# An attention and gated-convolution kernel: one convolution moved to other banks, one pair of loads moved forward, three output stores held back

## The chip, the cores and the metric

The kernel runs on one core of one Trainium2 chip. The metric is the device time of one execution in microseconds (us); the median of several executions is quoted, and a profile of one execution stands beside it. An execution counts as slow when it is over 1.5% above the fastest of the same kernel. Of all executions below only two of the kernel before, in the third call of the experiments (226.51 and 227.51 us), were slow; the ratios leave them out.

## The reference

Causal attention over 8 batches, 12 heads, 448 positions and 64 features per head, followed by a gated unit: a causal convolution of width 5 over each of the 768 features gives a gate, a dense product gives a value, and their product goes through an output projection.

```python
scores = scale * q @ k.T ; masked above the diagonal ; attn = softmax(scores)
x = (attn @ v) as [8, 448, 768]
gate = sigmoid(sum(conv_w[k] * x shifted by 4 - k for k in range(5)))
out  = (gate * (x @ w_val)) @ w_out        # float32 [8, 448, 768]
```

## The kernel before

The 96 heads are worked through as 24 groups of four (three groups to a batch). Everything is unrolled, and each engine is given its instructions in the order in which the program issues them. PSUM is the memory into which the matmuls write; the copy of a finished bank from there into an output tile, done by ACT, is called an eviction below. It is split by hand: two double banks for scores (`sc_ps`), two for attention values (`av_ps`), one for denominators (`den_ps`) and one more (`z_ps`); projections and value products borrow the last two.

```python
qk_pool = ctx.enter_context(tc.tile_pool(name="qk", bufs=QK_BUFS))     # 5
ob_pool = ctx.enter_context(tc.tile_pool(name="ob", bufs=4))           # output tiles
...
def load_v(n):            # on SP; buffer n % 3, so it waits for the cast of group n - 3
...
def conv(units, banks):   # 40 matmuls per group, then a tanh on ACT out of the banks
...
def project(p, m, half, o, tiles):
    if half == 0:
        obs[p, m] = ob_pool.tile([128, DM], FP32, name="ob")
    ob = obs[p, m]
    ...                                             # 6 or 24 matmuls into bank o
        nc.scalar.activation(out=ob[:, f], in_=o[:, 0:384], func=AF.Copy, scale=0.5)
    ...
    elif half == 1:
        nc.sync.dma_start(out=rows, in_=ob)         # 384 KB, on SP
...
def first_half(n):
    exps(n, 0)              # scores (PE), exponentials (ACT), masks (POOL)
    transposes(n + 1)       # q and k of the next group (DVE)
    cast_v(n)               # POOL
    load_v(n + 3)           # SP
    for m in {4: (6, 7), 5: (8,), 6: (9,), 7: (10, 11)}.get(n, (n + 4,)):
        load_qk(m)          # POOL's queue
...
for p in range(2, N // 2 + 1):        # two groups a turn; fill[] says how many
    n = 2 * p                         # half output tiles go into each gap
    first_half(n)
    gap(0, (den_ps, z_ps))
    second_half(n)                    # exps(n, 1)
    values(n - 1)                     # attention values (PE), normalisation (DVE)
    gap(1, (z_ps,), 4)
    ...
    first_half(n + 1)
    gap(2, (den_ps, z_ps))
    second_half(n + 1)
    if n < N:
        values(n)
    gap(3, (z_ps,), 4)
    conv((n - 2, n - 1) if p > 2 else (n - 1,), sc_banks)
    gap(4, (den_ps, z_ps, av_ps[0]))
```

In the turn p = 2 the gaps hold output tiles 0 and 1, in p = 3 tile 2, and in p = 4 tile 3's first half (gap 1), then tile 3's second half and tile 4's first half (both in gap 2), then tile 4's second half (gap 3).

The softmax here doesn't subtract the row's maximum and nothing guards it: scores larger than these inputs give would overflow.

## Time and profile before

| what | value |
|---|---|
| time, median of 3 runs (range) | 224.27 us (223.78 to 224.67) |
| span of the profiled execution | 222.6 us |
| TensorE busy | 208.4 us, 94% |
| idle of TensorE from 38.5 to 66.9 us | 2.9 us |
| idle of TensorE from 98 to 194 us | 0.1 us |
| ACT, DVE, POOL busy | 63%, 63%, 50% |

A busy share is an average over the whole span. What a change is worth is read from the stage that it touches: there TensorE either waits, and can gain, or it does not. The lines for this are in the prediction. In such lines PE is TensorE, ACT ScalarE, DVE VectorE, POOL GpSimd, and SPq the queue of SyncE, which issues the loads of v and all stores. The two leading numbers are the start and the duration in us, and a bracket gives an idle time of the engine and what ended it.

### The profile page before, as it was taken

How to read it: one execution, taken by the hardware profiler on the slowest of the kernel's cores; microseconds unless marked ns; L12 is line 12 of the kernel's file. 1: busy time of each engine (PE TensorE's matmuls, PEld its weight loads, DVE VectorE, ACT ScalarE, POOL GpSimd, SP SyncE). 2: the span in 40 equal slices, each digit the busy share in tenths (PEclk: the TensorE clock that was granted, in tenths of full speed). 3: DMA queues.
4: the chain of work that ended last, by engine and by line, in shares of the span. 5: the costliest groups of instructions: out<-in, count | busy, mean ns of one | idle time of the engine just before them, and what ended most of it. 6: DMA issues, size and time to landing. Idle time of an engine off the chain costs nothing.

```text
span 222.6 us, 8748 instructions
## 1 busy us (share of the span) xinstructions
PE 208.4 (94%) x3821; PEld 114.1 (51%) x3822; DVE 139.4 (63%) x251; ACT 139.7 (63%) x178; POOL 111.4 (50%) x192
## 2 busy tenths in 40 slices
PE   7997889987999999999999999999999999989992
PEld 3344434544455545545655655555555556546551
DVE  6747686558878754978828828749568476260400
ACT  2496316877666868667677777777677776406041
POOL 7299953893884736817717636557255155000000
PEclk9999699999999999999999999999999999999999
DMA  5999999899999885984885977758934210302333
GB/s 92 176 196 223 220 215 203 169 171 268 223 271 203 172 180 209 239 157 90 161 235 109 229 212 134 154 192 165 193 141 135 88 59 3 144 0 89 128 137 149
DMA packets 57696, 36.37 MB, mean 163 GB/s; under 512 B 46133, under 2 KB 54069, under 8 KB 57658
## 3 DMA queue, kind: packets, MB, share of 16 engines
q1 hardware_dynamic: 48922, 22.44, 37.6%
q0 software_dynamic: 8736, 13.37, 34.6%
q8 instruction: 30, 0.49, 0.9%
q14 instruction: 8, 0.07, 0.1%
HBM read 37.76 MB, written 11.01 MB: 219 GB/s over the span
## 4 chain that ended last, share of the span: by engine, by line
PE 77%; ACT 8%; DVE 7%; DMA 3%; issue 2%; POOL 1%; DVEq 0%; ACTq 0%; POOLq 0%
PE den_ps L263 12%; PE z_ps L263 11%; PE sc_ps L181 11%; PE z_ps L285 11%; ACT pt L190 7%; PE sc_ps L241 7%; PE den_ps L285 6%; PE av_ps L215 5%; PE den_ps L215 4%; PE av_ps L285 3%; PE z_ps L134 3%; DMA kb<-in_k_dram 3%; PE sc_ps L285 2%; DVE x L228 2%; DVE dt L222 1%
## 5 line engine op out<-in xcount | busy, mean ns | idle before, releaser
L190 ACT ACTIVATE pt<-sc_ps 128x1024 bf16<-128x1024 f32 x96 | 92.9, 1022 | 34.1 <-PE sc_ps L181 32.6
L194 POOL TENSOR_SCALAR_AFFINE_SELECT pt<-pt 128x512 bf16<-128x512 bf16 x24 | 16.0, 668 | 66.5 <-ACT pt L190 66.5
L285 PEld LDWEIGHTS <-gv 128*32 128x32 bf16 (+1 forms) x624 | 31.6, 97 | 22.3 <-issue 4.6
L263 PEld LDWEIGHTS <-wv 128*128 128x128 bf16 x288 | 26.4, 98 | 26.0 <-issue 3.2
L181 PE MATMUL sc_ps<-qt,kt 32*128 32x64 bf16 (+3 forms) x768 | 35.0, 277 | 2.1 <-ACT pt L190 1.6
L285 PE MATMUL z_ps<-wo,gv 128*32 128x384 bf16 (+1 forms) x462 | 33.2, 326 | 0.8 <-DVE gv L266 0.8
L200 POOL TENSOR_SCALAR_AFFINE_SELECT pt<-pt 128x512 bf16<-128x512 bf16 x48 | 30.2, 660 | 7.0 <-ACT pt L190 7.0
L181 PEld LDWEIGHTS <-kt 32*128 32x128 bf16 x768 | 18.4, 93 | 27.4 <-issue 17.2
L263 PE MATMUL z_ps<-x,wv 128*128 128x448 bf16 x138 | 30.2, 353 | 0.7 <-DVE x L228 0.7
L263 PE MATMUL den_ps<-x,wv 128*128 128x448 bf16 x138 | 30.3, 354 | 0.2
L266 DVE SCALAR_TENSOR_TENSOR gv<-gate,den_ps 128x448 bf16<-128x448 f32 x23 | 14.1, 612 | 24.6 <-PE den_ps L263 24.6
L228 DVE TENSOR_TENSOR x<-av_ps,rb 128x448 bf16<-128x448 f32 x48 | 27.7, 619 | 2.6
L248 ACT ACTIVATE gate<-sc_ps 128x896 f32<-128x896 f32 x23 | 19.9, 915 | 14.9 <-PE sc_ps L241 14.9
L222 DVE STREAM_TRANSPOSE dt<-den_ps 128x448 f32<-128x448 f32 x24 | 15.5, 644 | 18.4 <-PE den_ps L215 18.4
L215 PE MATMUL av_ps<-pt,vb 128*32 128x448 bf16 (+3 forms) x768 | 25.3, 274 | 0.7 <-DVE vb L86 0.7
L165 DVE STREAM_TRANSPOSE qt<-qb 128x448 uint32<-128x448 uint32 x24 | 22.8, 950 | 4.7 <-DMA qb<-in_q_dram 4.5
L290 ACT ACTIVATE ob<-z_ps 128x384 f32<-128x384 f32 x29 | 14.3, 493 | 15.8 <-PE z_ps L285 15.8
L165 DVE STREAM_TRANSPOSE kt<-kb 128x448 uint32<-128x448 uint32 x24 | 22.3, 930 | 1.8 <-DMA kb<-in_k_dram 1.8
L86 POOL CAST vb<-vf 128x1024 bf16<-128x1024 f32 x21 | 21.8, 1036 | 0.0
L215 PEld LDWEIGHTS <-vb 128*32 128x32 bf16 x768 | 16.3, 98 | 6.4 <-DVE vb L86 0.9
L241 PE MATMUL sc_ps<-x,cwd 32*32 32x448 bf16 x920 | 17.7, 369 | 1.8 <-DVE x L228 0.9
L266 DVE SCALAR_TENSOR_TENSOR gv<-gate,z_ps 128x448 bf16<-128x448 f32 x23 | 14.1, 614 | 7.9 <-PE z_ps L263 7.9
(46 smaller groups left out, 174.9 us busy)
## 6 DMA issues: line engine op xcount, KB each, us to landing
out_dram<-ob SPq DMA_DIRECT2D x27, 384.0 KB, 4.1
vf<-in_v_dram SPq DMA_DIRECT2D x72, 128.0 KB, 5.6
qb<-in_q_dram POOLq DMA_DIRECT2D x24, 224.0 KB, 4.8
kb<-in_k_dram POOLq DMA_DIRECT2D x24, 224.0 KB, 6.0
vf<-in_v_dram SPq DMA_DIRECT2D x24, 64.0 KB, 5.3
wv<-in_moe_w_val_dram POOLq DMA_DIRECT2D x12, 96.0 KB, 6.0
wo<-in_moe_w_out_dram POOLq DMA_DIRECT2D x6, 192.0 KB, 8.8
wv<-wv SPq DMA_DIRECT2D x4, 96.0 KB, 7.6
```

The source lines that it names most:

```text
L86: engine.tensor_copy(out=t, in_=vfs.pop(n))
L165: nc.vector.transpose(out=t.bitcast(U32).rearrange("p (b s) -> p s b", s=T), in_=qks.pop((name, n)).rearrange("p s d -> p (s d)").bitcast( ...
L181: nc.tensor.matmul(out=sc_ps[h // 2][:, h % 2, c0:c0 + nq], lhsT=kt[r, e, k0:k0 + 128], rhs=qt[r, e, q0:S], start=e == 0, stop=e == 1, ski ...
L190: nc.scalar.activation(out=pt[:, 2 * hp:2 * hp + 2, 512 * stage:512 * (stage + 1)], in_=sc_ps[hp], func=AF.Exp, scale=D ** -0.5)
L200: nc.gpsimd.affine_select(out=pt[:, :, c:c + 128], in_=pt[:, :, c:c + 128], compare_op=ALU.is_ge, fill=0.0, base=0, pattern=[[0, G], [1, 1 ...
L215: nc.tensor.matmul(out=o, lhsT=w, rhs=pt[:, h, col:col + nq], start=i == 0, stop=i == 3, skip_group_check=True, tile_position=(0, 32 * i_out))
L228: nc.vector.tensor_tensor(out=x[:, dh, 4:S + 4], in0=av_ps[dh][:, 0:S], in1=r, op=ALU.mult)
L241: nc.tensor.matmul(out=banks[u][i // 2][32 * j:32 * (j + 1), 0:S], lhsT=cwd[r, 2 * version(n) + dh, t], rhs=xs[n % 8][r, dh, t:t + S], sta ...
L248: nc.scalar.activation(out=gates[n], in_=sc_ps[u][:, :, 0:S], func=AF.Tanh, scale=0.5)
L263: nc.tensor.matmul(out=o[e][:, 0:S], lhsT=wv_sb[version(NG * b + cg)][:, ce, f:f + 128], rhs=xs[(NG * b + cg) % 8][:, ce, 4:S + 4], start= ...
L266: nc.vector.scalar_tensor_tensor(out=gv[g][:, e, S * (b % 2):S * (b % 2 + 1)], in0=gates[NG * b + g][:, e], scalar=1.0, in1=o[e][:, 0:S], ...
L285: nc.tensor.matmul(out=o[w * j:w * (j + 1), 0:384], lhsT=gvs[p][g][:, dh, 128 * m + w * j:128 * m + w * (j + 1)], rhs=wo_sb[c][:, f], star ...
```

## The change

Three things at once, all aimed at the early stage where TensorE still waits: the convolution of group 3 runs in the two value banks, ahead of group 4's values, so that the projection after it no longer needs `den_ps`; q and k of group 6 are asked for before a cast on POOL; and the stores of output tiles 0, 1 and 2 are held until tile 3 is complete, to leave the DMA queues to the loads.

```diff
@@ -271,6 +271,13 @@
     obs = {}
+    stores = []
+
+    def store():
+        while stores:
+            rows, ob = stores.pop(0)
+            nc.sync.dma_start(out=rows, in_=ob)
+
@@ -294,7 +301,9 @@
         elif half == 1:
-            nc.sync.dma_start(out=rows, in_=ob)
+            stores.append((rows, ob))
+            if p > 0 or m > 2:
+                store()
@@ -324,7 +333,7 @@
-            for m in {4: (6, 7), 5: (8,), 6: (9,), 7: (10, 11)}.get(n, (n + 4,)):
+            for m in {4: (7,), 5: (8,), 6: (9,), 7: (10, 11)}.get(n, (n + 4,)):
@@ -384,6 +393,7 @@
     conv((2,), [av_ps])
     exps(3, 1)
+    load_qk(6)
     cast_v(3)
@@ -412,11 +422,14 @@
         second_half(n + 1)
+        if p == 2:
+            conv((n - 1,), [av_ps])
         if n < N:
             values(n)
         gap(3, (z_ps,), 4)
-        conv((n - 2, n - 1) if p > 2 else (n - 1,), sc_banks)
-        gap(4, (den_ps, z_ps, av_ps[0]))
+        if p > 2:
+            conv((n - 2, n - 1), sc_banks)
+        gap(4, (den_ps, z_ps, av_ps[0]) if p > 2 else (z_ps,))
```

(Some unchanged lines around the edits are cut.)

## The prediction

> **What bounds the kernel now.** I read the page first: part 1 and the PE row of part 2.
>
> ```profile
> PE 208.4 (94%) x3821; PEld 114.1 (51%) x3822; DVE 139.4 (63%) x251; ACT 139.7 (63%) x178; POOL 111.4 (50%) x192
> ...
> PE   7997889987999999999999999999999999989992
> ```
>
> TensorE is busy for 208.4 of 222.6 us. The row shows that what it loses, it loses early (the first ten slices of 5.6 us) and in the tail. So a part of the change can gain only where TensorE waits early, and anything that stops TensorE in the dense middle is added in full.
>
> Second, the timeline of PE from 44 to 53 us, where groups 4 and 5 run and the convolution of group 3 stands:
>
> ```profile
> 46.88 0.63 PE L181 MATMUL sc_ps<-qt,kt 32*128 32x320 bf16 x14 [0.60 <-ACT pt L190]
> 47.44 0.62 PE L215 MATMUL den_ps<-pt,ones 128*32 128x448 bf16 x16
> 47.89 1.05 PE L215 MATMUL av_ps<-pt,vb 128*32 128x448 bf16 x32
> 48.87 1.14 PE L241 MATMUL sc_ps<-x,cwd 32*32 32x448 bf16 x40
> 51.21 1.14 PE L285 MATMUL den_ps<-wo,gv 128*128 128x384 bf16 x6 [1.20 <-DVE dt L222]
> 52.28 0.64 PE L181 MATMUL sc_ps<-qt,kt 32*128 32x448 bf16 x16
> ```
>
> One projection waits 1.20 us for the bank den_ps, because DVE had not yet read group 4's denominators. The timeline of DVE gives the reason:
>
> ```profile
> 48.37 0.98 DVE L165 STREAM_TRANSPOSE qt<-qb 128x448 uint32<-128x448 uint32 x1 [1.90 <-DMA qb<-in_q_dram]
> 49.75 0.95 DVE L165 STREAM_TRANSPOSE kt<-kb 128x448 uint32<-128x448 uint32 x1 [0.41 <-DMA kb<-in_k_dram]
> 50.56 0.60 DVE L222 STREAM_TRANSPOSE dt<-den_ps 128x448 f32<-128x448 f32 x1
> ```
>
> The transposes of group 6's q and k stand ahead of that read in DVE's order. They waited for loads that POOL issued only at 43.35 and 43.89, behind two casts. This is the wait the change aims at.
>
> Third, since held stores keep buffers, the timelines of ACT and then of SP at the place where the stores will now be issued:
>
> ```profile
> 75.36 0.50 ACT L290 ACTIVATE ob<-den_ps 128x384 f32<-128x384 f32 x1
> 75.73 0.51 ACT L290 ACTIVATE ob<-z_ps 128x384 f32<-128x384 f32 x1
> 76.12 1.95 ACT L190 ACTIVATE pt<-sc_ps 128x1024 bf16<-128x1024 f32 x2
> ```
>
> ```profile
> 77.61 2.00 SPq L78 DMA_DIRECT2D vf<-in_v_dram  x3
> 79.66 0.61 SPq L79 DMA_DIRECT2D vf<-in_v_dram  x1
> 80.80 2.69 SPq L297 DMA_DIRECT2D out_dram<-ob  x3
> ```
>
> By the plan of the loop, the evictions at 75.36 and 75.73 are the second half of output tile 3 and the first half of tile 4. The store of tile 3 was ready at 75.86, yet SP issued it at 80.80: it stood behind the loads of v for group 12, which wait for POOL's cast of group 9 (76.55 to 77.59 in the timeline of POOL).
>
> [...] a ready store stood 4.9 us behind a waiting load. [...] Here the store of 80.80 took 5.6 us to land, against a median of 4.1 for the 27 stores. [...] one ACT eviction that waits holds the exponentials behind it. No wait in this trace tests that on ACT; DVE shows the same (above). [...] The table by stage agrees: after TensorE had been only 0.29, 0.79, 0.56 and 0.40 busy in the four microseconds from 20 on, it shows
>
> ```profile
> 24.00:25.00 1.00, 1.00 (x48) 0.70 (x57) 1.00 (x1) 0.00 (x0) 1.00 (x3) 0.50 1.17 216
> 25.00:26.00 1.00, 1.00 (x43) 0.39 (x30) 0.00 (x0) 0.00 (x0) 1.00 (x2) 0.50 1.20 198
> 26.00:27.00 1.00, 1.00 (x27) 0.63 (x24) 0.00 (x0) 0.90 (x2) 1.00 (x3) 0.50 1.14 207
> ```
>
> The value 0.50 is the granted clock. Dense work resumed at 23.45 and the clock came back near 27.1, some 3.65 us later.
>
> **The change, part by part.** No arithmetic is added or removed.
>
> *q and k of group 6 sooner.* They go out after POOL's two masks that end at 35.45, in a stretch where POOL then waits 3.17 us for ACT, so issuing costs nothing. The buffers are free: five slots, and group 1 left its slot when its transposes ended near 13.5 us (timeline of DVE). Software-queue loads ahead of them land at about 1.4 us each (q and k of group 5 at 41.4 and 42.8), so I estimate 44.2 and 45.6. DVE is occupied until 46.47 with group 3's normalisation, so the transposes of group 6 follow without their 1.90 and 0.41 us waits. The DVE wait is removed.
>
> *Convolution of group 3 in the value banks, ahead of group 4's values.* The 40 matmuls (1.14 us) run at 47.44 to 48.55. Their gate activations queue behind the two exponentials on ACT (47.48 to 49.42) and take 0.49 each (the 0.98 for two in the convolution of group 2), ending at 49.92 and 50.41. Group 4's denominators run meanwhile (to about 49.05). Its two value products must wait for the banks, so they start at 49.95 and 50.45 and end at 50.88. This is a new wait of about 0.9 us. The projection after it now goes to z_ps, free since 42.1, and takes 0.97: scores of group 6 start at 51.85 in place of 52.28. **Gain: 52.28 - 51.85 = 0.43 us.** The old 1.20 is mostly exchanged for the new 0.9 plus a changed overlap.
>
> *Stores of tiles 0, 1, 2 held.* Before, they went out at 47.03, 57.08 and 61.62. Without them the early loads have somewhat less company; after 52 us no PE wait names a load, so I count no gain. But the output tiles have **four buffers**. Tiles 0 to 3 now fill all four, and tile 4's first eviction (75.73) needs the buffer of tile 0, whose store is issued only when tile 3 is complete and, in SP's order, after group 12's v. Worked out in the old times, then moved earlier by 0.43:
> - SP is free after its v loads at 80.27; I take 80.3 to 80.8 for the issue.
> - Landing: the store at 80.80 landed at 86.4, after the v pieces in front. The held one, up to 0.5 us sooner, at about 86.1.
> - ACT evicts tile 4 in 0.5 us: 86.6. The projection of tile 4's second half, also in z_ps, can then start.
> - TensorE had reached that point at 77.40 (scores of group 9 and values of group 8 do not need the evicted bank). **Stall: 86.6 - 77.4 = 9.2 us.** The shift of 0.43 moves both ends.
> - [...] the work that follows runs at half clock. The next projection (0.97) and the convolution of two groups (1.18) take 2.15 us at full clock. With 3.65 us at half clock they end 2.15 + 1.83 = 3.98 us after the restart; before it was 80.54 - 77.40 = 3.14. [...] **Clock: 0.8 to 2.4 us, taken as 1.5.** The exponentials held on ACT (1.95 us) lie beside the slow projection.
>
> From 98 to 194 TensorE idles 0.13 us in all, so nothing later takes this back. Sum: 224.3 - 0.4 + 9.2 + 1.5 = **234.6 us**, 4.6% slower.
>
> **Rivals.** *No buffer wait, only the intended gain:* if tile 4 found another buffer, or the store left before group 12's v, the result would be 223 to 224. For it speaks that the old trace shows no wait of ACT for a store; but there tile 0's store landed at 56.2, some 19 us before its buffer was wanted. Against it stand the four buffers and SP's order in the lines above. Chance 5%.
>
> *The wait is there but shorter:* a store landing in the median 4.1 us from 80.3 ends at 84.4, for a stall of 7.5 and little clock loss, 231.5 to 232. The lines of v in front speak against it. The opposite, a landing of 9.2 us as the first store had at 47.03, gives a stall of 13 and 239[...].
>
> *The freed DMA time speeds the early stage:* all PE idle between 38.5 and 66.9 is 2.9 us (0.48 + 0.70 + 1.20 + 0.29 + 0.20), so even a perfect gain leaves a net loss if the stall exists. If the stall does not exist and this holds, 221 to 222, still within 2%.
>
> **Range and chances.** The stall is certain to about nine in ten; its size rests on one landing time (one microsecond either way)[...], hence 231.3 to 237.6 around 234.6. Slower by over 2% means above 228.8, which every version with the stall gives: 0.93. Within 2%: 0.06. Faster by over 2% needs 4.5 us of gain where 2.9 of idle exists: 0.01.
>
> **What would show it.** Right: one ACT idle of some 9 to 10 us before an eviction of z_ps into ob, put down to the DMA of the output; one PE idle of about 9 us before a 24-matmul projection near 77 us, put down to that eviction; a granted clock near half for 3 to 7 us after it; four stores in a row on SP behind a v load; TensorE's busy time up by the half-clock time, 1 to 3 us. For the gain: transposes of group 6 without a DMA wait, no 1.20 us wait for den_ps, a new wait near 0.9 us of the value matmuls for gate activations. Wrong: no such ACT wait (rival one), or a first held store issued before 77 us.

## The result, and the profile after

The changed kernel takes 235.44 us (median of 6 runs, 233.86 to 236.23) against 224.25 us for the kernel before (6 runs). The ratio is 1.0486, with a 95% interval of 1.0445 to 1.0526. Here and below a ratio is the mean time of one kernel's fast runs over the mean of the other's fast runs of the same rounds, so it is not quite the ratio of the medians.

The profiled execution spans 232.1 us, 9.5 more than before. It was the quickest of the six, so the account below explains its 9.5 us and not the whole 11.2 between the medians. From the page, part 1 and two rows of part 2:

```profile
PE 209.5 (90%) x3821; PEld 114.8 (49%) x3822; DVE 140.7 (61%) x251; ACT 140.0 (60%) x179; POOL 111.2 (48%) x192
...
PE   7996889889999239999999999999999999999993
...
PEclk9999999999999957999999999999999999999998
```

A hole of two slices (2 and 3 tenths) has opened where the old row reads 9 throughout, and the granted clock falls in the two slices that follow its start (5 and 7 tenths). Nothing else of that size has changed.

**The early stage.** The timeline of PE where group 3's convolution now stands (times of start, duration, then what ended an idle time):

```profile
46.88 1.14 PE L241 MATMUL av_ps<-x,cwd 32*32 32x448 bf16 x40
...
49.34 1.06 PE L215 MATMUL av_ps<-pt,vb 128*32 128x448 bf16 x32 [0.78 <-ACT gate L251]
50.34 1.15 PE L292 MATMUL z_ps<-wo,gv 128*128 128x384 bf16 x6
51.42 0.63 PE L181 MATMUL sc_ps<-qt,kt 32*128 32x448 bf16 x16
```

The wait of 1.20 us for `den_ps` is gone, and a wait of 0.78 us for the gate activations has taken its place. Scores of group 6 start at 51.42 in place of 52.28. Of these 0.86 us, 0.53 were there already at the scores of group 5 (43.32 against 43.85), before the moved convolution runs. Over the thirteen profiles that start varies from 43.32 to 45.11, so the 0.53 are not credited to the change. From group 5 to group 6 it is 8.10 us against 8.43: 0.33 us gained. The timeline of DVE shows the same transposes as in the prediction (the read of group 4's denominators follows at 48.70):

```profile
45.85 0.96 DVE L165 STREAM_TRANSPOSE qt<-qb 128x448 uint32<-128x448 uint32 x1
46.66 0.94 DVE L165 STREAM_TRANSPOSE kt<-kb 128x448 uint32<-128x448 uint32 x1
```

They wait for no load any more; before the read DVE now waits 1.10 us for TensorE.

**The hole.** The timeline of ACT at tile 4:

```profile
84.35 0.49 ACT L297 ACTIVATE ob<-z_ps 128x384 f32<-128x384 f32 x1 [9.36 <-DMA out_dram<-ob]
```

ACT had evicted tile 3 by 74.99. Tile 4's first eviction waits 9.36 us for a store, and group 9's exponentials stand behind it and start at 84.74. The chain of waits shows how the store came to be so late:

```profile
75.69 1.05 POOL vb L86
...
78.63 0.61 SPq L79
...
79.33 4.93 DMA out_dram<-ob
```

POOL casts group 9's values, which frees a buffer for SP's four loads of v for group 12; the last of them is issued at 78.63; only then does SP reach tile 0's store, which needs 4.93 us to land. What TensorE does meanwhile is best seen side by side. Before:

```profile
77.40 1.15 PE L285 MATMUL z_ps<-wo,gv 128*32 128x384 bf16 x24
78.48 0.96 PE L241 MATMUL sc_ps<-x,cwd 32*32 32x448 bf16 x53
79.96 0.59 PE L241 MATMUL sc_ps<-x,cwd 32*32 32x448 bf16 x27 [0.51 <-issue]
80.47 1.15 PE L285 MATMUL den_ps<-wo,gv 128*128 128x384 bf16 x6
...
82.53 0.64 PE L181 MATMUL sc_ps<-qt,kt 32*128 32x448 bf16 x16
```

After:

```profile
84.89 2.11 PE L292 MATMUL z_ps<-wo,gv 128*32 128x384 bf16 x24 [8.18 <-ACT ob L297]
86.93 2.09 PE L241 MATMUL sc_ps<-x,cwd 32*32 32x448 bf16 x80
88.95 1.86 PE L292 MATMUL den_ps<-wo,gv 128*128 128x384 bf16 x6
...
91.72 0.64 PE L181 MATMUL sc_ps<-qt,kt 32*128 32x448 bf16 x16
```

The projection of 24 matmuls starts 7.49 us later although the program had run 0.86 us ahead, so the stall is 8.35 us. The same work then takes 6.83 us to the scores of group 10 (91.72 - 84.89) in place of 5.13 (82.53 - 77.40): 1.70 us more. From start to start the two projections on either side of the convolution take 2.04 and 1.70 us in place of 1.08 and 0.99. The convolution takes 2.02 in place of 1.99: before, TensorE stood idle for 0.51 us in the middle of it, with no cause that the profile shows, and the slower matmuls fill that time. The table by stage, of which the column before the last two is the granted clock, gives the reason for the slow matmuls:

```profile
80.00:81.00 1.00, 0.00 (x0) 0.00 (x0) 0.44 (x1) 0.00 (x0) 0.00 (x0) 0.59 1.13 205
...
90.00:91.00 1.00, 1.00 (x7) 0.51 (x6) 0.00 (x0) 1.00 (x3) 0.00 (x0) 0.79 0.06 12
```

Read in steps of 0.2 us, the step that ends at 80.20 shows 0.97, every one from there to 90.40 shows 0.50, and the next 0.93: the clock fell near 80.2 and came back near 90.4. The sum at group 10 is -0.86 + 8.35 + 1.70 = 9.19 us, and the whole span is 9.5 longer.

### The profile page after: what moved, and what is told of

Its sections match the earlier page's. It is cut to its first block, busy times and chain, and to the rows that moved or that the text cites. A ratio compares the mean times of both kernels' runs of the same rounds, so it can differ in the third digit from the quotient of the medians.

```text
span 232.1 us, 8754 instructions
## 1 busy us (share of the span) xinstructions
PE 209.5 (90%) x3821; PEld 114.8 (49%) x3822; DVE 140.7 (61%) x251; ACT 140.0 (60%) x179; POOL 111.2 (48%) x192
## 4 chain that ended last, share of the span: by engine, by line
PE 67%; DMA 9%; ACT 8%; POOL 7%; issue 3%; DVE 2%; SPq 1%; ACTq 0%; POOLq 0%; DVEq 0%
PE z_ps L292 11%; PE den_ps L263 10%; PE z_ps L263 10%; PE sc_ps L181 9%; DMA kb<-in_k_dram 7%; ACT pt L190 6%; PE sc_ps L241 6%; PE av_ps L215 5%; PE den_ps L292 4%; PE den_ps L215 3%; PE av_ps L292 3%; POOL wv L94 3%; PE sc_ps L292 2%; DMA out_dram<-ob 2%; PE z_ps L134 2%
## 5 line engine op out<-in xcount | busy, mean ns | idle before, releaser
L292 PEld LDWEIGHTS <-gv 128*32 128x32 bf16 (+1 forms) x624 | 32.1, 99 | 30.0 <-issue 12.1
L292 PE MATMUL z_ps<-wo,gv 128*32 128x384 bf16 (+1 forms) x468 | 35.3, 336 | 9.0 <-ACT ob L297 8.2
L297 ACT ACTIVATE ob<-z_ps 128x384 f32<-128x384 f32 x30 | 14.8, 492 | 27.3 <-PE z_ps L292 18.0
L248 ACT ACTIVATE gate<-sc_ps 128x896 f32<-128x896 f32 x22 | 19.0, 914 | 13.5 <-PE sc_ps L241 13.5
L241 PE MATMUL sc_ps<-x,cwd 32*32 32x448 bf16 x880 | 16.2, 372 | 1.5 <-DVE x L228 0.9
```

Source lines behind the costliest of these rows:

```text
L241: nc.tensor.matmul(out=banks[u][i // 2][32 * j:32 * (j + 1), 0:S], lhsT=cwd[r, 2 * version(n) + dh, t], rhs=xs[n % 8][r, dh, t:t + S], sta ...
L248: nc.scalar.activation(out=gates[n], in_=sc_ps[u][:, :, 0:S], func=AF.Tanh, scale=0.5)
L292: nc.tensor.matmul(out=o[w * j:w * (j + 1), 0:384], lhsT=gvs[p][g][:, dh, 128 * m + w * j:128 * m + w * (j + 1)], rhs=wo_sb[c][:, f], star ...
```

## The experiments

Theory: the whole loss is the wait for one of the four output buffers, made long by SP's order, with a clock penalty after it. Rivals: the burst of held stores costs by its traffic; the moved convolution or the earlier loads cost; the slow clock is hidden by ACT's backlog. Eleven kernels ran, in three calls, each beside the kernel before (medians 224.51, 224.55 and 224.98 us; the last is 224.55 without the two slow executions). All gave correct results.

| run | what it is | median us | ratio (95% interval) | longest ACT wait for a store, us |
|---|---|---|---|---|
| changed kernel | | 235.44 | 1.0486 (1.0445 to 1.0526) | 9.4 |
| hold alone | before + held stores | 234.25 | 1.0427 (1.0389 to 1.0466) | 9.4 |
| dummy matmuls | changed + 22 dummies in the stall | 234.06 | 1.0418 (1.0388 to 1.0448) | 9.4 |
| five buffers | changed | 231.49 | 1.0311 (1.0274 to 1.0349) | 4.5 |
| stores let go sooner | changed | 228.28 | 1.0188 (1.0120 to 1.0256) | 3.7 |
| six buffers | changed | 226.54 | 1.0083 (1.0043 to 1.0124) | 1.3 |
| eight buffers | changed | 225.35 | 1.0022 (0.9982 to 1.0062) | none |
| let go at tile 2 | changed | 224.96 | 1.0021 (0.9964 to 1.0079) | none |
| no hold | changed | 224.60 | 1.0002 (0.9967 to 1.0038) | none |
| convolution alone | before | 225.06 | 1.0014 (0.9973 to 1.0055) | none |
| q and k alone | before | 224.02 | 0.9967 (0.9926 to 1.0008) | none |
| q and k one step sooner | before | 224.29 | 1.0000 (0.9951 to 1.0050) | none |

**More output buffers.** Five, six and eight in place of four:

```diff
-    ob_pool = ctx.enter_context(tc.tile_pool(name="ob", bufs=4))
+    ob_pool = ctx.enter_context(tc.tile_pool(name="ob", bufs=5))     # also 6 and 8
```

> The changed kernel with five output tiles. Buffer theory: tile 5's first eviction, at about 81.4 us in the changed kernel's time, is now the one that needs tile 0's buffer, whose store lands at about 84.3. ACT waits 2.9 us in place of 9.4, TensorE idles under 3 us[...]: 226.3 us (ratio 1.009), clock 0.99. Rival (any wait for a store costs the whole stall, or traffic is the cause): 230 or more.

> The changed kernel with six output tiles in place of four. Buffer theory: the eviction of tile 4 finds a free buffer, ACT never waits for a store, and what is left is the gain of the first two parts: 223.4 us (ratio 0.994 to 0.999 to the kernel before), granted clock 0.99. Rival (the held stores cost by their burst of traffic at 79 us, or the moved convolution costs): still 230 or more, with the same late stores.

> The changed kernel with eight output tiles. The wait of ACT for a store was 9.4 us with four buffers, 4.5 with five, 1.3 with six. Buffer theory: none with eight, and 1.3 to 1.5 us less than six buffers: 225.0 us, the same within 0.3% as the run without the hold. Rival (the burst of held stores costs by its traffic): over 226 without any such wait.

The size of the loss follows the number of buffers: 9.4, 4.5, 1.3 and no ACT wait. The held stores leave at the same place in the program in all four, so their burst of traffic is there in the run with eight as well, and it costs nothing that the interval can see. That rival falls. My numbers were wrong for six and for five: 223.4 us expected and 226.54 measured, 226.3 expected and 231.49 measured. With six buffers I had expected no wait. The timeline of ACT shows one, before the first half of tile 6, too short to account for the 3.1 us that were missed; the rest has no explanation here:

```profile
87.37 0.49 ACT L297 ACTIVATE ob<-den_ps 128x384 f32<-128x384 f32 x1 [1.25 <-DMA out_dram<-ob]
```

Here tile 0's store left SP at 81.23 and took 6.1 us, not the 4.9 of the changed kernel. There TensorE, ACT, DVE and POOL were all idle from 81 to 84 us, while the table by stage gives a DMA share of 1.04 to 1.19 from 79 to 84 us; why the store landed sooner was not shown. With five I had expected 2.9 us of ACT wait and an undisturbed clock; the store took 6.4 us, ACT waited 4.5, TensorE 4.27, and the granted clock fell at about 87.8 and came back at about 91.2. The timeline of PE:

```profile
88.05 2.08 PE L292 MATMUL den_ps<-wo,gv 128*128 128x384 bf16 x6 [4.27 <-ACT ob L297]
```

**The hold alone.** The two edits around the stores on the kernel before, nothing else.

```diff
+            stores.append((rows, ob))
+            if p > 0 or m > 2:
+                store()
```

> The kernel before with only the stores of tiles 0 to 2 held. Theory: the whole loss is here, and the small gain of the other two parts is absent: 235.8 us, ratio 1.050 to 1.056, ACT waiting about 9 us for a store. Rival (the loss needs the moved convolution or the earlier q and k as well): within 1% of the kernel before.

Measured 1.0427, with a PE wait of 8.23 us. Nearly the whole loss is here; neither the convolution nor the earlier loads are needed for it. It is a little below the expected 1.050 to 1.056. In its one trace scores of group 6 follow those of group 5 after 7.88 us (before: 8.43), as the wait for `den_ps` shrank from 1.20 to 0.75 us. Group 6's loads were no sooner for it: DVE's transposes of them start at 48.37 and 49.67, before at 48.37 and 49.75. TensorE came to that place later (scores of group 5 at 44.32 and not 43.85) and so had less to wait.

**No hold, and letting go at tile 2.**

```diff
-            if p > 0 or m > 2:
-                store()
+            store()                     # no hold;  the other run: if p > 0 or m > 1
```

> The changed kernel without the hold: each of the first three tiles is stored as soon as it is complete, the moved convolution and the earlier q and k of group 6 stay, four buffers. Prediction's account: 0.4 us less than the kernel before, ratio 0.998, no ACT wait for a store. Rival: six buffers still gave 226.5, so the two other parts may cost about 1 us by themselves (the earlier loads delay q and k of group 5): ratio 1.003 to 1.006.

> The changed kernel, four buffers, with the stores let go when tile 2 is complete in place of tile 3: tiles 0 and 1 are still held, but the stores leave in the stage of group 6, some 10 us before any buffer is wanted again. Buffer theory: no ACT wait for a store, 224.6 us as without the hold, ratio 0.997 to 1.004. Rival (holding stores costs by bursts): slower by 1% or more.

Both are the kernel before within the intervals. A hold that ends one tile earlier is harmless: there SP issued the three stores from 59.59 us, over ten microseconds before a buffer was wanted again.

**Letting go sooner in the same turn.** The three held stores go right after tile 3's first half. On SP they then stand ahead of the v loads of group 12, not behind them.

```diff
+        if p == 0 and m == 3 and half == 0:
+            store()
```

> The changed kernel, four buffers, with one difference: the three held stores are let go right after tile 3's first half, so that on SP they stand ahead of the loads of v for group 12 and behind those of group 11. Order theory: the first held store leaves near 72.5 us in place of 79.3 and lands near 78, so ACT waits about 3 us in place of 9.4, TensorE loses about 2.5 us and no clock: 227 us, ratio 1.011. Rival (SP's order behind v does not matter, the buffer wait alone does): 233 or more.

The timeline of SP, then that of ACT:

```profile
74.13 1.65 SPq L279 DMA_DIRECT2D out_dram<-ob  x3
```

```profile
79.78 0.49 ACT L297 ACTIVATE ob<-z_ps 128x384 f32<-128x384 f32 x1 [3.71 <-DMA out_dram<-ob]
```

With the same four buffers the wait falls from 9.4 to 3.7 us, so SP's order behind v makes up over half of it. The store left at 74.13, not near 72.5, and the time is 228.28 us, more than the 227 expected. In part that is the clock, which fell here too, in an idle time of TensorE of only 2.54 us (77.79 to 80.32): from the restart to the scores of group 10 it is 5.74 us and not 5.13. The rest is not explained. The table by stage, which shows 0.50 for the three microseconds that follow:

```profile
79.00:80.00 1.00, 0.00 (x0) 0.00 (x0) 1.00 (x3) 0.22 (x1) 0.00 (x0) 0.96 1.03 415
```

**The clock by itself.** 22 useless matmuls into a value bank, in the stall.

```diff
+        if p == 4:
+            keep_clock(22, av_ps[0])
         gap(3, (z_ps,), 4)
```

> The changed kernel with 22 useless matmuls into a value bank in the stall (they start when group 8's normalisation has read that bank, near 78 us, and end near 83 us, before the stall does). The stall itself stays at 8.2 us between useful matmuls. Theory: the granted clock stays at 1.0 and the 1.7 us that half clock cost after the stall come back: 233.7 us (ratio 1.042). Rival (after the stall ACT's backlog sets the pace and the slow clock is hidden): 235.4 as the changed kernel.

The timeline of PE:

```profile
78.85 4.91 PE L134 MATMUL av_ps<-idle 128*128 128x512 bf16 x22 [1.64 <-DVE x L228]
85.41 1.16 PE L292 MATMUL z_ps<-wo,gv 128*32 128x384 bf16 x24 [1.65 <-ACT ob L297]
```

The ACT wait stays at 9.38 us, the granted clock is 1.00 throughout the stall, and the projection after it takes 1.16 us, not 2.11. The time falls to 234.06: 0.7% of the kernel before, about 1.5 us, against 1.7 expected. The two runs' intervals just meet (1.0448 and 1.0445), and the hold alone, with half clock in its trace, took no more than 234.25, so the times alone do not settle it. The trace does: from the restart to the scores of group 10 it is 5.05 us (85.41 to 90.46) in place of 6.83. The slow clock was not hidden by ACT.

The tables by stage, read in steps of 0.2 us, show more of the clock. Before the tail (from 220 us on) it is at half in ten of the thirteen profiles, for about 3.41 us at a time, once for 6.83, and for 10.24 in the two with a stall of over 8 us: one, two and three times 3.41. Between two such spells in the hold alone lie 54.61 us, 16 times 3.41. So the clock seems to be set anew at fixed steps of 3.41 us; this is inferred from these figures alone. In the run with the stores let go sooner the step that ended with the fall (76.50 to 79.92) held 1.29 us of matmuls, and the clock fell about 2.1 us after the last of them. Idle times of 1.64 and 1.65 us around the dummies, and one of 1.11 us in the run with six buffers, left the clock at 1.00. How much work in a step keeps the clock up was not shown.

**The first two parts, each alone.**

```diff
+    load_qk(6)             # ahead of cast_v(3); one step sooner: ahead of exps(3, 1)
-            for m in {4: (6, 7), 5: (8,), 6: (9,), 7: (10, 11)}.get(n, (n + 4,)):
+            for m in {4: (7,), 5: (8,), 6: (9,), 7: (10, 11)}.get(n, (n + 4,)):
```

These are the two edits of q and k alone, on the kernel before; the convolution alone is the last part of the change's diff.

> The kernel before with only the convolution of group 3 moved into the value banks (and the projection after it into z_ps). The 1.20 us wait for den_ps becomes a wait of about 0.8 us of the value products for the gate activations; scores of group 6 start some 0.4 us sooner: ratio 0.997 to 0.999. Rival: no change or slower, as the moved wait is as long as the old one.

> The kernel before with only the loads of group 6's q and k put ahead of the cast of group 3's values. The 1.20 us wait of a projection for den_ps falls away, and no wait for gate activations takes its place: about 1.0 us faster than the kernel before, ratio 0.994 to 0.997. Rival: the earlier loads share the queue with those of group 5 and only move the wait: ratio 1.000 or more.

> As the run with the earlier q and k alone, but the loads are asked for one step sooner still, right after the masks that end at 35.5 us (where the prediction had placed them; the changed kernel has them after the next masks, at 39.3). No wait is left there to remove, so the same as that run: ratio 0.994 to 0.999, scores of group 6 some 7.2 us after those of group 5. Rival: the loads delay group 5's q and k and the ratio is 1.000 or more.

By the measured times none of the three differs from the kernel before by more than its interval. The traces tell more about the place itself. From the scores of group 5 to those of group 6 it is 8.43 us before; 8.02 with the convolution alone, 8.02 with both and no hold (8.10 in the changed kernel), but 7.15 with q and k alone and 7.12 with them one step sooner. With q and k alone the timeline of PE shows the projection start without any wait:

```profile
49.52 1.15 PE L285 MATMUL den_ps<-wo,gv 128*128 128x384 bf16 x6
50.62 0.64 PE L181 MATMUL sc_ps<-qt,kt 32*128 32x448 bf16 x16
```

So the earlier loads alone remove the wait that both parts were meant to remove, and the moved convolution puts a 0.78 us wait in its place. That 1.3 us, 0.6%, should show in the time. In one run it may (0.9967), in the other it does not (1.0000). In several profiles, with the earlier loads and without, TensorE waits 0.2 to 0.6 us for output weights near 40 us, and the clock dips near 24 us in some (to 0.50 for 3.41 us in the kernel before) and not in others, so single executions differ by about as much as the gain. Whether q and k alone are faster stays open. No version was found that clearly beats the kernel before.

## Why the prediction was right

Predicted 234.6 us (231.3 to 237.6), measured 235.44.

- **The buffer wait**, the step on which all rested, holds: the wait scales with the number of buffers, is there with the hold alone, and is gone without it.
- **SP's order** holds: letting the stores stand ahead of group 12's v cut the wait from 9.4 to 3.7 us.
- **Size of the stall:** 9.2 us predicted, 8.35 measured. The term that was off is the landing: from the 5.6 us of a store in the kernel before I let the held store start at 80.3 and land at 86.1, 5.8 us, but the store for which everything waits took 4.9.
- **Clock:** 1.5 us predicted (0.8 to 2.4; only the lower end was worked out from a trace), 1.70 in the trace, about 1.5 by the run with dummy matmuls. The half clock lasted from the restart at 84.89 to about 90.4, 5.5 us, longer than the 3.65 worked out. The 3.65 was misread: it runs from 23.45, before the clock fell (23.8), to 27.1, where the return was at 27.2; the half clock itself lasted 3.4 us there. Nor was TensorE idle before that fall, but busy for 0.29 to 0.79 of each microsecond, so that a stall would bring the clock down was not shown by the trace before; the trace after shows it (0.50 from 80.2).
- **Gain of the first parts:** 0.43 us predicted, 0.33 in the trace (0.41 in two others); in the time nothing is visible. The predicted new wait of 0.9 us for gate activations measured 0.78.
- **An error in reading the diff**, as the prediction put it, "after POOL's two masks that end at 35.45": I placed the loads of group 6 after the masks that end at 35.45 us. They stand after the next masks, and POOL issued them at 39.27 and 39.81. They landed at 45.1 and 46.3, close to the 44.2 and 45.6 that I had estimated from an earlier issue, and in time for DVE; the run with the loads at the place that I had assumed shows the same stage. The mistake had no effect.
- **Nothing takes it back later:** from group 10 on the profile after is 0.3 us slower than the one before.
- **Some luck in the sum:** with the measured terms it is 224.3 - 0.33 + 8.35 + 1.70 = 234.0 us, which fits the profiled execution (233.86) and not the median. That 234.6 lies nearer to the median is owed to the landing that was taken too long.

What stays open: five of the six executions of the changed kernel took 1.1 to 2.4 us longer than the one that was profiled, and no profile shows which term grew in them.

## What to carry to other kernels

Holding a store holds its buffer: before delaying one, find the next writer of that buffer and ask when the store can have landed by then, counting what stands ahead of it on the issuing engine's queue. If the engine that then waits also feeds TensorE, look for a slow clock after the stall and add it to the cost (here the granted clock was 0.50 after idle times of TensorE of 8.18, 4.27 and 2.54 us, and cost 1.7 us after the first). And where two edits aim at one wait, try each alone: one may suffice and the other bring a wait of its own.
